# Operand addresses of four kinds of matmul products set congruent modulo 512 bytes

## The chip, the cores and the metric

The kernel runs on one core of one Trainium2 chip. The metric is device time in microseconds of one execution. The engines are TensorE (PE; its weight loads are listed apart as PEld), VectorE (DVE), ScalarE (ACT), GpSimd (POOL) and SyncE (SP, which issues DMAs). A tile lies on 128 partitions; an address here is the byte offset inside a partition of the on-chip memory (SBUF), and it is the same on all partitions.

## The reference

For tokens x (2048 x 512) the output is x + A(xn) + B(xn), where xn is the layer norm of x. A is linear attention with a learned feature map (32 heads of 16), B a gated unit whose gate mixes tokens:

```python
def _A_ref(x, wqkv, w_phi, wo):
    ...
    pq = jnp.einsum("bhsd,hdf->bhsf", q, w_phi)
    pk = jnp.einsum("bhsd,hdf->bhsf", k, w_phi)
    phi_q = jnp.concatenate([_softmax(pq, axis=-1), _softmax(-pq, axis=-1)], axis=-1)
    phi_k = jnp.concatenate([_softmax(pk, axis=-1), _softmax(-pk, axis=-1)], axis=-1)
    kv = jnp.einsum("bhsf,bhsd->bhfd", phi_k, v)
    z  = jnp.einsum("bhsf->bhf", phi_k)
    num = jnp.einsum("bhqf,bhfd->bhqd", phi_q, kv)
    den = jnp.einsum("bhqf,bhf->bhq", phi_q, z)[..., None] + 1e-6
    o = num / den
    return (...) @ wo

def _B_ref(x, w_in, w_sp, b_sp, w_out):
    z = _gelu(jnp.einsum("bsd,df->bsf", x, w_in))
    z1 = z[..., :Fh]
    z2 = _layernorm(z[..., Fh:], axis=-1)
    g = jnp.einsum("ts,bsf->btf", w_sp, z2) + b_sp[None, :, None]
    return jnp.einsum("bsf,fd->bsd", z1 * g, w_out)
```

w_in is 512 x 1376 (Fh = 688), w_sp 2048 x 2048, w_out 688 x 512.

## The kernel before

All is float32. Each product is made of three matmuls on operands split into a high and a low part: `mm3` (lines 51 to 55) issues ah·bh, ah·bl and al·bh, which are the rows of L53, L54 and L55. The first operand of a matmul is loaded as weights (128 columns), the second is streamed (344 or 512 columns). There are 16 tiles of 128 tokens.

*Phase 0* (to about 205 us). For each tile, x is centred and transposed, and split into xT (high and low); `proj` multiplies xT with wv and with wqk (q and k), 4 chunks of 128 rows each, 512 columns. A softmax pair on DVE and ACT makes e; `add_kv` adds the products of e and v into kvps (L312) after the tiles in RUNS. `z1_raw` multiplies xT with the first half of w_in (w1: two halves of 344 columns, each as h and l) into zps.

*Phase 1* (to about 284 us). The last five tiles of z1 follow; `make_zb` sums zacc over the tokens with four matmuls (pz, from zh and zl); `load_win` loads and splits the second half of w_in (w2), eight chunks of 344 columns; then z2 = xT · w2 for 16 tiles, gelu and norm, and `b_split` turns each pair of token tiles into B tiles (with sums in a tile T of the pool zw, one buffer).

*The gate's products* (to about 495 us). 32 steps of w_sp times z2 in a seven-product form (FORM: P1, P2, P6, P5, P7, P3, P4), 42 matmuls of 344 columns per step. `prep_a` prepares a step's weights: it loads wf, makes four sums in a tile S (lines 531 to 535) and splits wf and S into A tiles. After every fourth step `drain` reads the seven sums out, and the result goes through `gate` to u.

*Phase 2*. For each tile, u times w_out (wu, 512 columns, five chunks and a rest), the attention (`attend`), and its product with wo (four chunks), both into pout.

The order of instructions on each engine is set by the framework's scheduler, by its own estimate of times, among what the data, the buffers and a few explicit `issue_after` permit. So a change of buffers can move instructions that the diff does not name. SP issues its DMAs in order: one that waits for a buffer holds up those behind it.

*Addresses.* The pool xz has 16 slots of P x 2 x FH floats (5504 bytes, 10 times 512 and 384 more). xT, B, wu, u and staged tiles lie in them, so that tiles in neighbouring slots differ by 384 modulo 512, and the low half of an xT lies 2752 bytes (192 modulo 512) behind the high one. A chunk of w1 or w2 is 344 floats, 1376 bytes (352 modulo 512). The chunks of xT (128 floats) and of wv, wqk and wo (512 floats) are multiples of 512 bytes. wo's product has its two operands at the constant difference 192, the projections have one of 0, 128, 256 and 384 by tile, the wu product 128, 256 or 384 (once 0), the z and g products each of the 16 multiples of 32.

Of the kernel before, what the change touches and what calls it, by code (L numbers as in the profile page):

```python
# [10 lines left out]
F32 = mybir.dt.float32  # L11
F32R = mybir.dt.float32r
# [6 lines left out]
P = 128  # L19
# [12 lines left out]
XB = 5  # L32
NP = NT // 2
HP, QP = P // 2, P // 4


@with_exitstack
def mixer(ctx: ExitStack, tc: tile.TileContext, x, x_t, wv, wqkT, phi_bd, wo, w_in, wst, b_r, w_out, out):
# [25 lines left out]

    cst = ctx.enter_context(left("cst", 1))
    xz = ctx.enter_context(left("xz", NT))
    mid = ctx.enter_context(ExitStack())
    dram = ctx.enter_context(tc.tile_pool(name="dram", bufs=1, space=DRAM))
    e_d = dram.tile([NT, P, NF + 2 * H], F32, name="e_d")
# [96 lines left out]
    with ExitStack() as p0:  # L166
# [11 lines left out]
        wqk_h = res.tile([P, 2, ND, D], F32R, name="wqk_h")  # L178
        wqk_l = res.tile([P, 2, ND, D], F32R, name="wqk_l")
        def stage(name, dt=F32):  # L180
            return xz.tile([P, 2, FH], dt, tag="xz", name=name)

        def split_w(h, l, src, t):
            sp.dma_start(t, src)
            round_h(act, h, t)
            rest_l(l, t, h)

        bd = stage("bd")[:, 0, :D]

        def load_rows(src):  # L190
            raw = [stage("wrow") for _ in range(2)]
# [29 lines left out]
            return [[pl.tile([P, D], F32, tag=tag, name="fold").rearrange("p (c g b) -> p c g b", c=2, g=NG)  # L221
                     for _ in range(2)] for pl, tag in pools]

        w1 = [[w1_pool.tile([P, ND, FC], F32R, name=f"w1_{j}{k}") for k in "hl"] for j in range(2)]

        def load_win(dst, j, stp, tag, bufs):
            for c in range(ND):
                t = stp.tile([P, D if tag == "x" else FC], F32, tag=tag, bufs=bufs, name="wst_")
                split_w(dst[0][:, c], dst[1][:, c], w_in[c * P:(c + 1) * P, j * FC:(j + 1) * FC], t[:, :FC])

        def proj(s, wh, wl, p=None, cs_=range(ND)):
            p = ps.tile([P, D], F32, tag="mm", name="proj") if p is None else p
# [9 lines left out]
                xt[s] = load_x(s)  # L242

        def split_x(src):
            t = xz.tile([P, 2, FH], F32R, tag="xz", name="xT")
            xT.append(t)
            src = src.rearrange("p a b -> p (a b)")
            rounded.append(round_h(act, t[:, 0, :D], src))
            return rounded[-1], rest_l(t[:, 1, :D], src, t[:, 0, :D])

        def stats(s, keep=lambda **ins: None):
            st6 = wk.tile([P, 6], F32, tag="st6", name="st6")
# [35 lines left out]

        def proj_k(s):
            er = spare[s].rearrange("p a b -> p (a b)")[:, :NF + 2 * H] if s in spare else None  # L290
            return softmax_pair(wk, proj(s, wqk_h[:, 1], wqk_l[:, 1]), "k", r_x[:, s:s + 1], ebufs=3, er=er)

        def proj_q(s):
            e = softmax_pair(wk, proj(s, wqk_h[:, 0], wqk_l[:, 0]), "q", r_x[:, s:s + 1])
# [27 lines left out]
        wkT_t = load_rows.raw  # L322
        fetch(2)
        wqT = load_rows(wqkT[:D])
        fetch(3)
        w1r = [stage("w1row") for _ in range(2)]
        for c in range(ND):
# [39 lines left out]
            keep(act=i, dve=j)  # L367


        t = xz.tile([P, 2, FH], F32R, tag="xz", name="xT")  # L370
        xT.append(t)
        x0, pts = xt.pop(0), []
        for k in range(2):
# [56 lines left out]
                    keep(act=round_h(act, h, src))  # L430
                    keep(dve=rest_l(l, src, h))

        ek = [softmax_pair(wk, p, "k", r_x[:, 0:1], ebufs=3, meanwhile=split_w1)]
        proj_v(2)
        keep(pe=proj.last)
        ek.append(proj_k(1))
# [1 line left out]
        split_x(turned(3))  # L438
        z1_raw(wk, za, 0, 2)
        keep(pe=zproj.last)  # L440
        spare.update(zip((3, 4, 8, 9), wkT_t + w1r))
        n1, nq = 1, 0
        for s in range(NT):
            fetch(s + 4)
# [25 lines left out]
    ctx_zw, ctx_w2 = right("zw", 1), right("w2", 1)  # L470
    zw = ctx_zw.__enter__()
    w2_pool = ctx_w2.__enter__()
    w2 = [[w2_pool.tile([P, ND, FC], F32R, name=f"w2_{j}{k}") for k in "hl"] for j in range(2)]
    zbp_ctx = psum("zb", 1)
    zbp = zbp_ctx.__enter__()

# [40 lines left out]
    def prep_a(n, f):  # L517

        a, b = f
        pl = hl[n % 2]  # L520
        ops = {}

        def parts(names, src):
            t = pl.tile([P, 2, len(names), 2, P], F32R, tag="".join(names), name="A")
            prep_a.last = b_parts(t[:, 0], t[:, 1], src)
            for k, m in enumerate(names):
                ops[m] = t[:, 0, k], t[:, 1, k]

        sums = ws.tile([P, 4, 2, P], F32, tag="S", name="S")
        parts(("A11", "A12"), a)  # L530
        dve.tensor_tensor(sums[:, 0], b[:, 0], b[:, 1], op=ALU.add)
        dve.tensor_tensor(sums[:, 1], sums[:, 0], a[:, 0], op=ALU.subtract)  # L532
        parts(("S1", "S2"), sums[:, 0:2])
        dve.tensor_tensor(sums[:, 2], a[:, 0], b[:, 0], op=ALU.subtract)
        dve.tensor_tensor(sums[:, 3], a[:, 1], sums[:, 1], op=ALU.subtract)
        parts(("S3", "S4"), sums[:, 2:4])
        parts(("A22",), b[:, 1:2])
        return ops

    hl, raw, A = [ws, None], {}, {}  # L540
    NE = 2
    with ExitStack() as p1:
        tmp1 = p1.enter_context(left("tmp1", 1))
        kvT = tmp1.tile([P, D], F32, name="kvT")
        zb = tmp1.tile([P, NF], F32, name="zb")
        psk = p1.enter_context(psum("psk", 2))

        def make_zb():

            ones_r = tmp1.tile([P, P], F32R, name="ones_r")  # L550
            round_h(act, ones_r, ones)
            for k in range(2):
                pz = psk.tile([P, D], F32, tag="kvt", name="pz")
                cs = slice(k * D, (k + 1) * D)
                h, l = (tmp1.tile([P, D], F32R, tag="z" + n, bufs=2, name="z" + n) for n in "hl")
                round_h(act, h, zacc[:, cs])
                rest_l(l, zacc[:, cs], h)
                pe.matmul(pz, ones_r, h, start=True, stop=False)
                pe.matmul(pz, ones_r, l, start=False, stop=True)
                dve.tensor_copy(zb[:, cs], pz)  # L560

        def make_kvT():
            kvm = zw.tile([P, 4, FC], F32, tag="T", name="kvm").rearrange("p a b -> p (a b)")[:, :D]
            kvm = kvm.rearrange("p (g b) -> p g b", b=P)
            dve.tensor_tensor(kvm.rearrange("p g (k b) -> p g k b", k=2),
                              kv_acc.unsqueeze(2).to_broadcast([P, NG, 2, HP]),
                              mask.rearrange("p (k b) -> p k b", k=2).unsqueeze(1).to_broadcast([P, NG, 2, HP]),
                              op=ALU.mult)
            pt = psk.tile([P, NG, P], F32, tag="kvt", name="kvt")
            for g in range(NG):  # L570
                pe.transpose(pt[:, g], kvm[:, g], ident)
            act.activation(kvT, pt.rearrange("p g b -> p (g b)"), AF.Copy)

        with ExitStack() as p1a:
            ta = p1a.enter_context(left("tmp1a", 1))
            for j in range(2):
                load_win(w2[j], 2 + j, ta, "st", 4)
            for s in range(NT - LAG, NT):
                z1_raw(tmp1, (za, zbp)[s % 2], s, 2)
                if s == NT - LAG + 1:  # L580
                    make_zb()
            make_kvT()
            raw[0], raw[1] = load_a(0), load_a(1)
            A[0] = prep_a(0, raw.pop(0))
        sp.dma_start(kvT_d, kvT)
        sp.dma_start(zb_d, zb)
        tb = p1.enter_context(left("tmp1b", 1))
        for s in range(NE):
            et = load_q(s, tb.tile([P, QW], F32, tag="et", bufs=2, name="et"))
            tmp = zw.tile([P, 4, FC], F32, tag="z2", bufs=2, name="qtmp").rearrange("p a b -> p (a b)")[:, :NF]  # L590
            e, _ = q_fin(et, tmp, zb)
            early = sp.dma_start(e_d[s, :, :NF], e).ins
# [12 lines left out]
    def b_tile():  # L605
        nonlocal nb
        k, nb = nb, nb + 1
        shape = [P, 2, 2, FC]
        if k < 10:
            return (xz2a if k < 5 else xz2).tile(shape, F32R, tag="b", name="B")  # L610
        if k < 26:
            return xz.tile(shape, F32R, tag="xz", name="B")
        return x3[0].tile(shape, F32R, tag="b", name="B")

    B, b11 = [], None

# [60 lines left out]
    raw[2] = load_a(2)  # L677
    normed(*late.pop(), ins)
    ctx_zw.__exit__(None, None, None)
    ctx_zc.__exit__(None, None, None)  # L680
    zbp_ctx.__exit__(None, None, None)
    ctx_z.__exit__(None, None, None)
# [60 lines left out]
        return turn  # L743

    def slot(name, dt=F32):
        return xz.tile([P, 2, FH], dt, tag="xz", name=name).rearrange("p a b -> p (a b)")

    def load_w(src, parts, h, l, t):
        rows = 0
# [16 lines left out]
        return ap.rearrange("p (k b) -> p k b", b=P)  # L766

    def first_gate(i):
        a, b = slot("u_uh", F32R), slot("ul_rt", F32R)
        n = KF * P  # L770
        u = load_u(i, k_tiles(a[:, :n]).bitcast(F32), b[:2 * REM, n:n + P])
        return split_u(*u, k_tiles(a[:, n:2 * n]), k_tiles(b[:, :n]))

# [5 lines left out]
        return e  # L779

    def stage_w():
        t = [xz2.tile([P, 2, 2, FC], F32, tag="b", name="wof").rearrange("p a b c -> p (a b c)") for _ in range(3)]
        w = [slot("wu", F32R) for _ in range(KF + 1)]
        for c in range(KF + 1):
            n = P if c < KF else 2 * REM
            h, l = (w[c][:n, k * D:(k + 1) * D] for k in range(2))
            rows = [(c * P, (c + 1) * P)] if c < KF else [(KF * P, FH)] * 2
            load_w(w_out, rows, h, l, t[c // 2][:, c % 2 * D:(c % 2 + 1) * D])
            wu.append((h, l))

    g, es, ets = {}, {}, {}
    for n in range(NC):
# [26 lines left out]
            es[2], last = q_fin(ets.pop(2), slot("qtmp")[:, :NF], zb)  # L819
        if n == NC - 2:  # L820
            es[0], es[1] = first_q(0), first_q(1)
            t = slot("u1", F32R)
            us = {1: load_u(1, k_tiles(t[:, :KF * P]).bitcast(F32), t[:2 * REM, KF * P:(KF + 1) * P])}
    cb = drain(NP - 1, g, slot("c").rearrange("p (k j f) -> p k j f", k=2, j=2))
    with tc.issue_after(cb[2]):
# [109 lines left out]

    fT = attend_T(0)
    wk.tile([P, D], F32, tag="xr", bufs=3, name="xr")
    wk.tile([P, 40], F32, tag="gap", name="gap")
    wk.tile([P, NG, 2 * P], F32R, tag="oTh", name="oT")
    with tc.issue_after(lasts[5]), tc.issue_after(lasts[1]), tc.issue_after(fin[-1]):  # L940
        for c in range(ND):
# [79 lines left out]
```

## Time and profile before

| | us |
|---|---|
| median of 3 runs | 631.67 (630.98 to 631.93) |
| the profiled execution | 632.01 |
| its span | 629.9 |
| PE busy | 623.2 |
| DVE busy | 508.3 |
| ACT busy | 278.8 |
| POOL busy | 102.8 |

In a row of a group stand the line, the engine, the operation, output and inputs by the program's names without numbers, shapes and count, then busy time in us and the mean of one in ns, then idle time in front of it. In a row of the timeline stand start and duration in us. The duration of a matmul is modelled and longer than the time to the next one's start, since they overlap; times of matmuls are therefore taken from start to start. In a row of windows stand the window, its length, the busy time and number of instructions of each engine, the granted clock of TensorE (1.00 is full speed), the busy share of the DMA engines and GB/s. In a row of waits stand the instruction, what it waited for, the total in us, how often, and the longest.

### The profile page before, as it was taken

The numbers are of one execution on the slowest core, as the hardware profiler recorded it, in microseconds if no ns is written. First come the engines' busy times: TensorE is split into PE (matmuls) and PEld (weight loads), VectorE is DVE, ScalarE is ACT, GpSimd is POOL, SyncE is SP. The second block draws the span as 40 slices with busy tenths as digits, with TensorE's granted clock in tenths as the row PEclk, the third lists the DMA queues.
The fourth block names the chain that finished last, engine by engine and source line by source line (L and its number), as shares of the span: only waits on it lengthen the run. The fifth ranks groups of instructions, "written<-read, shape, count | busy, mean of one in ns | idle before, by whom it ended". The sixth has DMA issues, their size and how long they took to land.

```text
span 629.9 us, 11435 instructions
## 1 busy us (share of the span) xinstructions
PE 623.2 (99%) x4406; PEld 566.0 (90%) x4406; DVE 508.3 (81%) x893; ACT 278.8 (44%) x446; POOL 102.8 (16%) x187
## 2 busy tenths in 40 slices
PE   8999999999999999999999999999999999999997
PEld 7888888888888999999999999999999877777785
DVE  5999998988997669889989697696969899989211
ACT  5653434343332637887534344243444433334331
POOL 3142121110111005432000000000000212211110
PEclk9999999999999999999999999999999999999999
DMA  9445455345335957102463745637377799984822
GB/s 316 153 114 142 112 151 146 109 131 142 107 92 163 287 195 263 55 2 68 128 140 122 177 92 154 133 117 170 88 184 231 226 295 332 329 229 110 160 33 52
DMA packets 87590, 98.40 MB, mean 156 GB/s; under 512 B 46560, under 2 KB 59616, under 8 KB 87296
## 3 DMA queue, kind: packets, MB, share of 16 engines
q1 hardware_dynamic: 75200, 58.12, 33.0%
q0 software_dynamic: 10032, 33.92, 20.6%
q10 hardware_dynamic: 2304, 5.64, 2.4%
q8 instruction: 34, 0.56, 0.4%
q14 instruction: 20, 0.16, 0.1%
HBM read 56.37 MB, written 30.54 MB: 138 GB/s over the span
## 4 chain that ended last, share of the span: by engine, by line
PE 97%; DVE 1%; DMA 1%; issue 0%; POOL 0%; DVEq 0%; POOLq 0%
PE g L53 10%; PE g L55 10%; PE g L54 10%; PE proj L53 7%; PE proj L55 7%; PE proj L54 7%; PE zps L53 6%; PE zps L55 6%; PE zps L54 6%; PE pout L53 5%; PE pout L55 5%; PE pout L54 5%; PE ptq L879 1%; PE po L894 1%; PE kvps L312 1%; PE pout L908 1%
## 5 line engine op out<-in xcount | busy, mean ns | idle before, releaser
L54 PE MATMUL g<-B,A 128*128 128x344 f32 x448 | 143.2, 320 | 0.0
L53 PE MATMUL g<-B,A 128*128 128x344 f32 x448 | 143.1, 320 | 0.0
L55 PE MATMUL g<-B,A 128*128 128x344 f32 x448 | 142.9, 320 | 0.0
L53 PEld LDWEIGHTS g<-B,A 128*128 128x128 f32 x448 | 84.2, 188 | 0.0
L54 PEld LDWEIGHTS g<-B,A 128*128 128x128 f32 x448 | 84.2, 188 | 0.0
L55 PEld LDWEIGHTS g<-B,A 128*128 128x128 f32 x448 | 84.1, 188 | 0.0
L45 ACT ACTIVATE A<-S 128x512 fp32r<-128x512 f32 x64 | 39.3, 628 | 78.7 <-DVE S L532 60.2
L113 ACT ACTIVATE e<-e,r_x 128x1024 f32<-128x1024 f32 x28 | 32.2, 1149 | 47.1 <-DVE e L112 46.7
L53 PE MATMUL proj<-wqk_h,xT 128*128 128x512 f32 x128 | 50.9, 398 | 0.0
L55 PE MATMUL proj<-wqk_h,xT 128*128 128x512 f32 x128 | 50.6, 395 | 0.0
L54 PE MATMUL proj<-wqk_l,xT 128*128 128x512 f32 x128 | 50.3, 393 | 0.0
L49 DVE TENSOR_TENSOR A<-S,A 128x512 fp32r<-128x512 f32 x64 | 43.1, 685 | 6.5 <-ACT A L45 6.3
L45 ACT ACTIVATE A<-wf 128x512 fp32r<-128x512 f32 x64 | 33.3, 520 | 29.3 <-PE g L55 17.8
L53 PE MATMUL zps<-w_0h,xT 128*128 128x344 f32 x128 | 41.4, 323 | 0.0
L55 PE MATMUL zps<-w_0h,xT 128*128 128x344 f32 x128 | 41.1, 321 | 0.0
L53 PE MATMUL zps<-w_1h,xT 128*128 128x344 f32 x128 | 41.0, 320 | 0.0
L55 PE MATMUL zps<-w_1h,xT 128*128 128x344 f32 x128 | 40.9, 320 | 0.0
L54 PE MATMUL zps<-w_0l,xT 128*128 128x344 f32 x128 | 40.9, 319 | 0.0
L54 PE MATMUL zps<-w_1l,xT 128*128 128x344 f32 x128 | 40.9, 319 | 0.0
L116 DVE TENSOR_REDUCE sm<-e 128x64 f32<-128x1024 f32 x28 | 33.8, 1208 | 5.4 <-ACT e L113 5.4
L49 DVE TENSOR_TENSOR A<-wf,A 128x512 fp32r<-128x512 f32 x64 | 35.1, 548 | 3.1 <-ACT A L45 3.1
L696 POOL DMA_DIRECT2D z1t<-z_d x16 | 8.6, 544 | 165.1 <-DMA u_d<-z1t 127.5
(208 smaller groups left out, 1428.2 us busy)
## 6 DMA issues: line engine op xcount, KB each, us to landing
wf<-in_wst SPq DMA_DIRECT2D x64, 256.0 KB, 3.5
e_d<-e POOLq DMA_DIRECT2D x16, 544.0 KB, 5.4
et<-e_d SPq DMA_DIRECT2D x16, 544.0 KB, 6.2
zacc<-e POOLq DMA_DIRECT2D x12, 512.0 KB, 4.6
er<-et POOLq DMA_DIRECT2D x12, 512.0 KB, 5.5
z_d<-z1f ACTq DMA_DIRECT2D x16, 344.0 KB, 3.1
z1t<-z_d POOLq DMA_DIRECT2D x16, 344.0 KB, 5.1
u<-u_d SPq DMA_DIRECT2D x15, 320.0 KB, 5.2
```

Source lines behind the costliest of these rows:

```text
L45: return act.activation(h, src, AF.Copy).ins
L49: return (eng or dve).tensor_tensor(l, src, h.bitcast(F32), op=ALU.subtract).ins
L53: pe.matmul(dst, ah, bh, start=start, stop=False)
L54: pe.matmul(dst, ah, bl, start=False, stop=False)
L55: return pe.matmul(dst, al, bh, start=False, stop=stop).ins
L113: act.activation(e, e, AF.Exp, scale=scale)
L116: dve.tensor_reduce(sm, heads(e), axis=AX.X, op=ALU.add)
L312: i = pe.matmul(kv_acc[k:k + QP, m // 4], vs[:, m * QP:(m + 1) * QP], e[:, m * HP:(m + 1) * HP], start=first and m < 4 and len(ready) == n ...
L696: pool.dma_start(t[:, k, :FH], z1_d[2 * i + k])
L879: pe.transpose(pt[:, a, k].bitcast(F32R), src, ident_r)
L894: lasts[3] = pe.matmul(po[r][c * QP:(c + 1) * QP, k], kvT[rows, m // 2, cols], fs[m // 4][rows, m // 2 % 2], start=True, stop=True).ins
L908: lasts[2] = pe.matmul(p, rt, w, start=False, stop=i == NT - 1 and k == 1).ins
```

## The change

It sets the address differences of the operands of four kinds of products (projections, z, wu, wo) to multiples of 512 bytes:

- the slots of xz, and of the pools for B and for staged w_out, get 5632 bytes (11 times 512); the low half of an xT follows its high half after 2048 bytes;
- each chunk of w1 and w2 gets 384 floats of room, 1536 bytes, of which 344 are used;
- a small tile is put behind w2, and the one called gap in front of oT grows from 40 to 64 floats.

To make room for it,

- S shares the slot of T (tag "T" of zw, one buffer) for the first two steps, and gets a pool of its own behind that;
- the w2 chunks are staged in tiles of tag "z2", four to a tile;
- zh and zl become one tile zhl, which the first et later takes the place of;
- the ring of e for k has two buffers instead of three, and three more tiles use spare slots of xz.

The B operands of the g products keep their inner layout; with slots of 5632 bytes their differences to A are 448, 352, 288 and 0 for the high part, and 192 more for the low one.

```diff
+FP = 3 * P
+SL = 2 * FH + QP
...
+    def xz_tile(n, dt, name):
+        return xz.tile([P, SL], dt, tag="xz", name=name)[:, :n]
...
-        w1 = [[w1_pool.tile([P, ND, FC], F32R, name=f"w1_{j}{k}") for k in "hl"] for j in range(2)]
-
-        def load_win(dst, j, stp, tag, bufs):
+        w1 = [[w1_pool.tile([P, ND, FP], F32R, name=f"w1_{j}{k}")[:, :, :FC] for k in "hl"] for j in range(2)]
+
+        def load_win(dst, j):
+            t = zw.tile([P, 4, FC], F32, tag="z2", bufs=2, name="wst_")
             for c in range(ND):
-                t = stp.tile([P, D if tag == "x" else FC], F32, tag=tag, bufs=bufs, name="wst_")
-                split_w(dst[0][:, c], dst[1][:, c], w_in[c * P:(c + 1) * P, j * FC:(j + 1) * FC], t[:, :FC])
+                split_w(dst[0][:, c], dst[1][:, c], w_in[c * P:(c + 1) * P, j * FC:(j + 1) * FC], t[:, c])
...
-            t = xz.tile([P, 2, FH], F32R, tag="xz", name="xT")
+            t = xz_tile(2 * D, F32R, "xT").rearrange("p (a b) -> p a b", a=2)
             xT.append(t)
             src = src.rearrange("p a b -> p (a b)")
-            rounded.append(round_h(act, t[:, 0, :D], src))
-            return rounded[-1], rest_l(t[:, 1, :D], src, t[:, 0, :D])
+            rounded.append(round_h(act, t[:, 0], src))
+            return rounded[-1], rest_l(t[:, 1], src, t[:, 0])
...
-            return softmax_pair(wk, proj(s, wqk_h[:, 1], wqk_l[:, 1]), "k", r_x[:, s:s + 1], ebufs=3, er=er)
+            return softmax_pair(wk, proj(s, wqk_h[:, 1], wqk_l[:, 1]), "k", r_x[:, s:s + 1], er=er)
...
-        spare.update(zip((3, 4, 8, 9), wkT_t + w1r))
+        spare.update(zip((2, 3, 4, 5, 8, 9), [bd_t] + wkT_t + wqT_t[:1] + w1r))
...
-    w2 = [[w2_pool.tile([P, ND, FC], F32R, name=f"w2_{j}{k}") for k in "hl"] for j in range(2)]
+    w2 = [[w2_pool.tile([P, ND, FP], F32R, name=f"w2_{j}{k}")[:, :, :FC] for k in "hl"] for j in range(2)]
+    w2_pool.tile([P, QP], F32, name="gap")
...
-        sums = ws.tile([P, 4, 2, P], F32, tag="S", name="S")
+        sums = (sm[0].tile([P, 4, 2, P], F32, name="S") if sm else
+                zw.tile([P, 4, FC], F32, tag="T", name="S").rearrange("p a b -> p (a b)")[:, :8 * P].rearrange("p (a k b) -> p a k b", a=4, k=2))
...
+        zhl = tmp1.tile([P, 4, D], F32R, tag="zhl", name="zhl")
...
-                h, l = (tmp1.tile([P, D], F32R, tag="z" + n, bufs=2, name="z" + n) for n in "hl")
+                h, l = (zhl[:, 2 * k + n] for n in range(2))
...
-            et = load_q(s, tb.tile([P, QW], F32, tag="et", bufs=2, name="et"))
+            et = load_q(s, tb.tile([P, QW], F32, name="et") if s else tmp1.tile([P, 4, D], F32, tag="zhl", name="et").rearrange("p a b -> p (a b)")[:, :QW])
...
-        shape = [P, 2, 2, FC]
         if k < 10:
-            return (xz2a if k < 5 else xz2).tile(shape, F32R, tag="b", name="B")
-        if k < 26:
-            return xz.tile(shape, F32R, tag="xz", name="B")
-        return x3[0].tile(shape, F32R, tag="b", name="B")
+            t = (xz2a if k < 5 else xz2).tile([P, SL], F32R, tag="b", name="B")
+        elif k < 26:
+            t = xz_tile(SL, F32R, "B")
+        else:
+            t = x3[0].tile([P, SL], F32R, tag="b", name="B")
+        return t[:, :4 * FC].rearrange("p (a b c) -> p a b c", a=2, b=2)
...
     ctx_zw.__exit__(None, None, None)
+    sm.append(mid.enter_context(right("S", 1)))
...
-        w = [slot("wu", F32R) for _ in range(KF + 1)]
+        w = [xz_tile(2 * D, F32R, "wu") for _ in range(KF + 1)]
...
-    wk.tile([P, 40], F32, tag="gap", name="gap")
+    wk.tile([P, 2 * QP], F32, tag="gap", name="gap")
```

No engine gets more or fewer instructions. Three places move.

SP, at the end of phase 0 (wst is the staging of w2, wf the weights of a gate step, et the stored features of q). Before:

```order
L173 DMA xt<-in_x 128x512 x12
L184 DMA wst__2248<-in_w_in 128x344
L184 DMA wst__2260<-in_w_in 128x344
L513 DMA wf<-in_wst 128x512 x3
L184 DMA wst__2264<-in_w_in 128x344
L184 DMA wst__2276<-in_w_in 128x344
L513 DMA wf<-in_wst 128x512
L586 DMA zb_d<-zb 128x1024
L513 DMA wf<-in_wst 128x512 x2
L480 DMA et<-e_d 128x1088 x2
```

(between wst__2248 and wst__2260, and between wst__2264 and wst__2276, two more like them). After:

```order
L179 DMA xt<-in_x 128x512 x12
L489 DMA et<-e_d 128x1088 x2
L190 DMA wst__2245<-in_w_in 128x344 x4
L190 DMA wst__2258<-in_w_in 128x344 x4
L522 DMA wf<-in_wst 128x512 x4
L595 DMA zb_d<-zb 128x1024
```

The two loads of et stand ahead of the eight of w2 instead of behind them, and the loads of wf behind all of these.

DVE, where the sums of the second gate step, A[1], are made. Before they stand right behind the last splits of w2 (S_3262 is their tile):

```order
L49 TENSOR_TENSOR w2_1l_2233<-wst__2272,w2_1h_2232 128x344
L49 TENSOR_TENSOR w2_1l_2233<-wst__2276,w2_1h_2232 128x344
L531 TENSOR_TENSOR S_3262<-wf_2456 128x256
L534 TENSOR_TENSOR S_3262<-wf_2454,wf_2456 128x256
L532 TENSOR_TENSOR S_3262<-S_3262,wf_2454 128x256
L535 TENSOR_TENSOR S_3262<-wf_2454,S_3262 128x256
L487 TENSOR_TENSOR qtmp_2483<-et_2481,zb_2241 128x1024
```

After (S_3248 is their tile, T_3224 the one whose slot it takes, A_3254 and A_3259 what is split from it) they stand at the end of the z2 stage:

```order
L639 TENSOR_TENSOR T_3224<-z2_3080,T_3224 128x344
L51 TENSOR_TENSOR B_3234<-T_3224,B_3234 128x688
L51 TENSOR_TENSOR A_3353<-wf_3265,A_3353 128x512
L51 TENSOR_TENSOR B_3226<-z2_3173,B_3226 128x344
L51 TENSOR_TENSOR B_3237<-T_3224,B_3237 128x688
L51 TENSOR_TENSOR B_3275<-z2_3173,B_3275 128x688
L541 TENSOR_TENSOR S_3248<-wf_2443 128x256
L544 TENSOR_TENSOR S_3248<-wf_2441,wf_2443 128x256
L542 TENSOR_TENSOR S_3248<-S_3248,wf_2441 128x256
L545 TENSOR_TENSOR S_3248<-wf_2441,S_3248 128x256
L51 TENSOR_TENSOR A_3254<-S_3248,A_3254 128x512
L51 TENSOR_TENSOR A_3259<-S_3248,A_3259 128x512
```

The four sums moved behind the last reader of T_3224.

PE, at steps 1 and 2 of the gate's products; of each product (six matmuls) the first row is shown. Before, step 1 runs P1, P2, P6, P5, P7, P3, P4:

```order
L53 MATMUL g_3310<-B_2814,A_3263 128x344
L53 MATMUL g_3317<-B_2818,A_3263 128x344
L53 MATMUL g_3324<-B_2825,A_3268 128x344
L53 MATMUL g_3331<-B_2822,A_3268 128x344
L53 MATMUL g_3338<-B_2822,A_3273 128x344
L53 MATMUL g_3345<-B_2818,A_3273 128x344
L53 MATMUL g_3352<-B_2825,A_3276 128x344
```

After (g_3299, g_3306 and g_3341 are P1, P2 and P4; g_3313, g_3320, g_3327 and g_3334 are P6, P5, P7 and P3):

```order
L55 MATMUL g_3299<-B_2800,A_3249 128x344
L55 MATMUL g_3306<-B_2804,A_3249 128x344
L55 MATMUL g_3341<-B_2811,A_3262 128x344
L55 MATMUL g_3299<-B_2989,A_3353 128x344
L55 MATMUL g_3306<-B_2993,A_3353 128x344
L55 MATMUL g_3341<-B_3000,A_3366 128x344
L55 MATMUL g_3313<-B_2811,A_3254 128x344
L55 MATMUL g_3320<-B_2808,A_3254 128x344
L55 MATMUL g_3327<-B_2808,A_3259 128x344
L55 MATMUL g_3334<-B_2804,A_3259 128x344
```

P1, P2 and P4 of step 2 (A_3353, A_3366) now run ahead of P6, P5, P7 and P3 of step 1, which need the sums; from there to about step 5 products are taken in pieces, those on high parts first.

More of the change, by code (lines that the diff above doesn't have):

```diff
@@ L180, in stage @@
         def stage(name, dt=F32):
-            return xz.tile([P, 2, FH], dt, tag="xz", name=name)
+            return xz_tile(2 * FH, dt, name).rearrange("p (a b) -> p a b", a=2)
         def split_w(h, l, src, t):
@@ L186, in split_w @@
             rest_l(l, t, h)
-        bd = stage("bd")[:, 0, :D]
+        bd_t = stage("bd")
+        bd = bd_t[:, 0, :D]
         def load_rows(src):
@@ L324, in mixer @@
         wqT = load_rows(wqkT[:D])
+        wqT_t = load_rows.raw
         fetch(3)
@@ L367, in split_t @@
             keep(act=i, dve=j)
-        t = xz.tile([P, 2, FH], F32R, tag="xz", name="xT")
+        t = xz_tile(2 * D, F32R, "xT").rearrange("p (a b) -> p a b", a=2)
         xT.append(t)
@@ L431, in split_w1 @@
                     keep(dve=rest_l(l, src, h))
-        ek = [softmax_pair(wk, p, "k", r_x[:, 0:1], ebufs=3, meanwhile=split_w1)]
+        ek = [softmax_pair(wk, p, "k", r_x[:, 0:1], meanwhile=split_w1)]
         proj_v(2)
@@ L538, in prep_a @@
         return ops
-    hl, raw, A = [ws, None], {}, {}
+    hl, raw, A, sm = [ws, None], {}, {}, []
     NE = 2
@@ L572, in make_kvT @@
             act.activation(kvT, pt.rearrange("p g b -> p (g b)"), AF.Copy)
[L574 to L584, printed above, removed]
+        for j in range(2):
+            load_win(w2[j], 2 + j)
+        for s in range(NT - LAG, NT):
+            z1_raw(tmp1, (za, zbp)[s % 2], s, 2)
+            if s == NT - LAG + 1:
+                make_zb()
+        make_kvT()
+        raw[0], raw[1] = load_a(0), load_a(1)
+        A[0] = prep_a(0, raw.pop(0))
         sp.dma_start(kvT_d, kvT)
@@ L745, in slot @@
     def slot(name, dt=F32):
-        return xz.tile([P, 2, FH], dt, tag="xz", name=name).rearrange("p a b -> p (a b)")
+        return xz_tile(2 * FH, dt, name)
     def load_w(src, parts, h, l, t):
@@ L768, in first_gate @@
     def first_gate(i):
-        a, b = slot("u_uh", F32R), slot("ul_rt", F32R)
         n = KF * P
+        a, b = xz_tile(2 * n, F32R, "u_uh"), xz_tile(n + P, F32R, "ul_rt")
         u = load_u(i, k_tiles(a[:, :n]).bitcast(F32), b[:2 * REM, n:n + P])
@@ L781, in stage_w @@
     def stage_w():
-        t = [xz2.tile([P, 2, 2, FC], F32, tag="b", name="wof").rearrange("p a b c -> p (a b c)") for _ in range(3)]
-        w = [slot("wu", F32R) for _ in range(KF + 1)]
+        t = [xz2.tile([P, SL], F32, tag="b", name="wof") for _ in range(3)]
+        w = [xz_tile(2 * D, F32R, "wu") for _ in range(KF + 1)]
         for c in range(KF + 1):
@@ L821, in mixer @@
             es[0], es[1] = first_q(0), first_q(1)
-            t = slot("u1", F32R)
+            t = xz_tile((KF + 1) * P, F32R, "u1")
             us = {1: load_u(1, k_tiles(t[:, :KF * P]).bitcast(F32), t[:2 * REM, KF * P:(KF + 1) * P])}
```

## The prediction

> **What bounds the kernel now.** I read the page's busy times first, then the waits of TensorE, then the matmul groups, then start-to-start times in the timeline.
>
> ```profile
> span 629.9 us, 11435 instructions
> PE 623.2 (99%) x4406; PEld 566.0 (90%) x4406; DVE 508.3 (81%) x893; ACT 278.8 (44%) x446; POOL 102.8 (16%) x187
> PE idle L340 <- POOL ident masks.py:199: 1.8, 1, 1.8
> PE ptq L879 <- DVE c L714: 0.2, 1, 0.2
> ```
>
> PE is busy 99% of the span, and the last two rows are all that PE waited for: 2.0 us. So only two things can shorten this kernel: fewer columns (the change removes none) or a shorter time from one matmul's start to the next. And any new wait in front of PE is paid in full. Which matmuls does the change touch?
>
> ```profile
> L53 PE MATMUL proj<-wqk_h,xT 128*128 128x512 f32 x128 | 50.9, 398 | 0.0
> L53 PE MATMUL proj<-wv_h,xT 128*128 128x512 f32 x64 | 25.9, 404 | 0.0
> L53 PE MATMUL zps<-w_0h,xT 128*128 128x344 f32 x128 | 41.4, 323 | 0.0
> L53 PE MATMUL pout<-wu,uh 128*128 128x512 f32 x75 | 30.7, 410 | 0.0
> L53 PE MATMUL pout<-woh,oT 128*128 128x512 f32 x60 | 23.7, 396 | 0.0
> L53 PE MATMUL g<-B,A 128*128 128x344 f32 x448 | 143.1, 320 | 0.0
> ```
>
> Each row has two like it, for L54 and L55, and w_0h one for w_1h (buffer numbers are left out in names). So the projections are 3 x 192 = 576 matmuls, z is 3 x 2 x 128 = 768, wu 3 x 80 = 240 (with five triples of the first tile, in another group), wo 180, and g 1344. The mean of one (320 or 398 ns) is no price: its end is modelled. The price is the start-to-start time:
>
> ```profile
> 310.00:490.00 180.00, 180.00 (x1146) 1.00 0.58 145
> 225.48 0.32 PE L53 MATMUL zps<-w_1h,xT 128*128 128x344 f32 x1
> 284.04 0.32 PE L53 MATMUL g<-B,A 128*128 128x344 f32 x1
> 110.95 0.39 PE L53 MATMUL proj<-wv_h,xT 128*128 128x512 f32 x1
> 113.71 0.39 PE L53 MATMUL proj<-wqk_h,xT 128*128 128x512 f32 x1
> ```
>
> In the g stage 180 us hold 1146 matmuls, 157 ns each, at a granted clock of 1.00. From the second to the third row lie 372 z matmuls: 58.56 / 372 = 157.4 ns. A projection tile of 12 matmuls of 512 columns takes 2.76 us, 230.0 ns each.
>
> [...]
>
> **Does the start-to-start time depend on addresses?** Per triple (ah·bh, ah·bl, al·bh) I sorted the times by the residue modulo 512 bytes between the streamed operand and the loaded one, by the addresses that the pools give.
>
> ```profile
> 43.24 0.32 PE L53 MATMUL zps<-w_1h,xT 128*128 128x344 f32 x1
> 43.70 0.39 PE L53 MATMUL proj<-wqk_h,xT 128*128 128x512 f32 x1
> 280.26 0.32 PE L53 MATMUL zps<-w_1h,xT 128*128 128x344 f32 x1
> 280.72 0.32 PE L53 MATMUL zps<-w_1h,xT 128*128 128x344 f32 x1
> ```
>
> These are the first and last of the 15 undisturbed z triples at residue 0 (each row pair is one triple, 0.46 us). Their mean is 466.9 ns; residue 256 gives 468.0 (14 triples), residue 32 the worst, 475.4 (16), and all 228 together 472.2. So for 344 columns congruence is worth 5.3 ns per triple. For 512 columns it is hardly visible:
>
> ```profile
> 176.69 0.40 PE L53 MATMUL proj<-wqk_h,xT 128*128 128x512 f32 x1
> 179.46 0.40 PE L53 MATMUL proj<-wqk_h,xT 128*128 128x512 f32 x1
> 595.00 0.39 PE L53 MATMUL pout<-wu,uh 128*128 128x512 f32 x1
> 597.79 0.39 PE L908 MATMUL pout<-wu,rt 96*128 96x512 f32 x1
> 573.53 0.40 PE L55 MATMUL pout<-woh,oT 128*128 128x512 f32 x1
> 576.80 0.29 PE L879 MATMUL ptq<-zb,er 128*128 128x128 f32 x2
> ```
>
> A projection tile at residue 0 takes 2.77 us (230.8 ns each); the tile at residue 384 above took 230.0, all tiles average 231.2. Twelve wu matmuls (residues 256, 128, 256, 384) take 2.79 us (232.5 each), and 14 wo matmuls, all at the constant residue 192, 3.27 us (233.6 each). Single steps run from 0.22 to 0.24 us.
>
> **The change part by part.** *z* (w1 and w2 chunks 1536 bytes apart, h and l apart by a multiple of 512): all 16 residues become 0. 256 triples x 5.3 ns = 1.36 us; in those 15 triples the residual part was not at 0, which is at 0 now, so I take **-1.5**. Ends: -4.9 (the shortest single step, 0.15 us, for all 768: 768 x 6.4 ns) and +0.8 (the worst residue: 256 x 3.2 ns).
>
> *Projections*: from 231.2 to the residue-0 tile's 230.8, 576 x 0.4 = **-0.2**. Ends: -4.1 (0.224 each) and +1.4 (wo's 233.6).
>
> *wu*: from 232.5 towards 230.8, 240 x 1.7 = -0.4; the row at residue 0 is a projection's, so I take **-0.3** (ends -2.0 and +0.3). *wo*: from 233.6 to 230.8, 180 x 2.8 = **-0.5** (ends -1.7 and 0).
>
> *g*: the B tiles' slots grow to 5632 bytes, which leaves four residues (448, 352, 288, 0, each with its l part) instead of 16. The triples of g at those four cost 469.3, 474.8, 473.2 and 473.6, mean 472.7, against 472.2 for all 443: 448 x 0.5 = **+0.2** (ends -1.3 and +1.2, by the best and worst residue, 469.3 and 474.8).
>
> *S shares the slot of T* until step 2. Before, the sums of A[1] were made early, in a pause of VectorE, and their lows at 287.49:
>
> ```profile
> 221.73 0.42 DVE L531 TENSOR_TENSOR S<-wf 128x256 f32<-128x256 f32 x1
> 285.67 0.88 DVE L620 TENSOR_TENSOR T<-z 128x688 f32<-128x688 f32 x1
> 286.46 0.69 DVE L49 TENSOR_TENSOR A<-wf,A 128x512 fp32r<-128x512 f32 x1
> 287.06 0.51 DVE L624 TENSOR_TENSOR T<-z,T 128x344 f32<-128x344 f32 x1
> 287.49 1.28 DVE L49 TENSOR_TENSOR A<-S,A 128x512 fp32r<-128x512 f32 x2
> 288.70 0.42 DVE L49 TENSOR_TENSOR A<-wf,A 128x256 fp32r<-128x256 f32 x1
> 289.03 0.51 DVE L629 TENSOR_TENSOR T<-z,T 128x344 f32<-128x344 f32 x1
> 289.46 0.87 DVE L49 TENSOR_TENSOR B<-z,B 128x688 fp32r<-128x688 f32 x1
> 290.24 0.42 DVE L531 TENSOR_TENSOR S<-wf 128x256 f32<-128x256 f32 x1
> 290.58 0.42 DVE L534 TENSOR_TENSOR S<-wf 128x256 f32<-128x256 f32 x1
> 305.00 0.46 ACT L715 ACTIVATE c<-g 128x344 f32<-128x344 f32 x1 [0.48 <-PE g L55]
> ```
>
> VectorE runs here without a gap; from start to start a T takes 0.79 or 0.43, A<-wf 0.60 or 0.33, A<-S 0.60, a B 0.78 (0.43 for half), a sum 0.34. Now the four sums of A[1] stand behind the T readers of b_split(6). From T at 285.67 its order has three T, three A<-wf, five B, the four sums with an A<-wf, two A<-S: 1.65 + 1.53 + 3.55 + 1.70 + 1.20 = 9.6 us, so A[1]'s lows are done at 295.3. PE takes it up by running P1, P2 and P4 of steps 1 and 2 first, and asks for them 78 matmuls after 284.04, at 296.3: no wait. A[2]'s lows stand behind c, which waits for PE's own P1 and P2 of step 3 (117 matmuls after 284.04, done at 302.7) and ACT's copy (0.46): with c (0.50), a sum and A<-S they are there at 304.6. PE asks for the first of them after 124 matmuls, at 303.5. That is **+1.1**; ends 0 (c later in VectorE's order than A<-S) and 4 (the four sums, two A<-S, a T and a B all in front of PE). Queued behind that A<-S are VectorE's sums for step 3, for which PE waits next; the loads of wf on SP that wait for the S of A[1] come later too, but VectorE reaches them later still.
>
> *SP*: the two et loads come ahead of all eight w2 chunk loads, and et(0) now waits for zhl's readers.
>
> ```profile
> 198.51 0.33 SPq L184 DMA_DIRECT2D wst__2248<-in_w_in  x1
> 211.59 0.39 PE L559 MATMUL pz<-zl,ones_r 128*128 128x512 f32 x1
> 211.80:225.50 13.70, 13.70 (x90) 13.65 (x89) 10.16 (x23) 8.67 (x19) 0.00 (x0) 1.00 0.95 314
> 223.51 0.40 PE L53 MATMUL zps<-w_0h,xT 128*128 128x344 f32 x1
> ```
>
> So the w2 loads can't start before about 211.8 (211.59 is the last matmul that reads zhl), where the first started at 198.51. Two et (544 KB each), eight chunks (172 KB) and three z_d writes (344 KB) are 3.6 MB, at 314 GB/s 11.4 us: landed by 223.2, split a microsecond later. PE needs the first half at 223.5 and the second at 225.48; the second is 1.3 us early, the first some 2 us. **0**, ends 0 and 3.4 (with half of the bandwidth, SP's 2.5 MB take 16 us, and the second half is split at 228.9).
>
> *The ring of e* drops from three buffers to two: e(14) then waits for the kvps matmuls that read the buffer before it, and VectorE's softmax with it; four PSUM buffers of projections cover that for PE. **0**, up to 1 if PE ran out of those buffers. The split of w1 writes the same elements, and phase 2's order of loads changes by a place or two: **0**, PE waits for none of them now.
>
> Sum: -1.5 - 0.2 - 0.3 - 0.5 + 0.2 + 1.1 = **-1.2 us** on the profiled execution's 632.01 (span 629.9, 2.1 around it), which is 0.34 above the median; on the median 631.67 it gives **630.5**.
>
> **The rivals.** *Floors* (0.15): every congruent matmul reaches the shortest steps seen, 0.15 and 0.22 us. 4.9 + 4.1 + 2.0 + 1.7 = 12.7 saved less 1.3: 620.3; half of it, 626.6. For it: equal residues repeat their steps to a nanosecond or so, so the spread is no noise. Against: short steps of 512 columns are followed by long ones, and no tile lies under 230.0.
>
> *Addresses do nothing* (0.15): the spread is timing, and z's gain at residue 0 goes when every neighbour is alike. Then g's place and S's wait remain: 633.0. [...]
>
> *A uniform residue locks into a bad pattern* (0.15), the one that ends slower: wo is the one product with one residue throughout, and it alternates 0.236 and 0.231, the worst of the 512s. If residue 0 does so too, the projections pay 576 x 2.4 = 1.4, wu 240 x 1.1 = 0.3, z the worst residue's 0.8, wo nothing, with g and S 1.3: +3.8, 635.5. It decides once a 512-column step passes about 231.8.
>
> *A new wait in front of PE* (0.13): w2's second half behind et (up to 3.4 us at 225.5) or S at its upper end (4 at 303), with the address gains kept: 631.9 to 633.9. For it: the DMA engines are 0.95 busy in that stretch. Against: 1.3 us of slack.
>
> **How the numbers follow.** The forecast has 0.42 and lies at 629 to 632. From no change 0.2% (1.26 us, about what a measurement can tell here) is easily missed: of its 0.42 some 0.27 is faster, 0.14 the same, 0.01 slower. Floors are faster (0.15). Nothing: 0.10 same, 0.05 slower. Lock: slower but for 0.02. New wait: 0.05 same, 0.08 slower. In all 0.42 faster, 0.31 same, 0.27 slower. The range 625.0 to 634.8 leaves out the lower half of the floors and the upper half of the lock.
>
> **What would show it.** In the after profile the first and last rows of z's stage should lie 372 x 1.9 = 0.7 us closer; wo's 14 matmuls should take 3.23 us instead of 3.27; a wait of PE on A<-S near 303 of about 1 us, none at 223 to 226. Wrong if the congruent 512s leave the band of 230 to 232.5, if z's triples don't get under 468, or if the list of PE's waits has more than 2 us of new ones.

## The result and the profile after

The changed kernel takes 642.87 us (median of 6 runs, 641.82 to 643.65) against 631.56 (630.98 to 631.93): a ratio of 1.0178, 95% interval 1.0165 to 1.0192. Forecast were 630.5 us and a range up to 634.8. The profiled execution has a span of 640.2 us, 10.3 more than before. Of all executions below, one of f4_x3_kvt was disturbed (granted clock 0.85, 678.16 us) and is left out.

The page of the changed kernel: span, busy times, and of the 40 slices the rows of PE and of its granted clock.

```profile
span 640.2 us, 11431 instructions
PE 621.8 (97%) x4406; PEld 565.1 (88%) x4406; DVE 508.8 (79%) x893; ACT 280.6 (44%) x446; POOL 104.6 (16%) x187
PE   8999999999999999999999999999999399999997
PEclk9999999999999999999999999999999799999999
```

PE is busy 1.4 us less than before, in a span that is 10.3 longer. The loss lies in one slice, the 32nd (496 to 512 us), where PE is busy three tenths and its clock falls. The list of PE's waits (us in total, times, longest) names it:

```profile
PE po L905 <- ACT f L892: 9.7, 1, 9.7
PE idle L348 <- POOL ident masks.py:199: 1.8, 1, 1.8
PE g L55 <- ACT A L47: 1.1, 1, 1.1
PE pout L57 <- DVE oT L51: 0.4, 1, 0.4
PE proj L55 <- ACT wv_h L47: 0.3, 1, 0.3
PE zps L55 <- ACT z1f L149: 0.3, 1, 0.3
```

One wait of 9.7 us, of the attention product po on f, the transposed features that ScalarE copies out of PSUM. Which instruction of ScalarE was late, and for what? The timelines of PE, ScalarE and GpSimd of the changed kernel around that place:

```profile
500.51 0.64 PE L905 MATMUL po<-f,kvT 64*32 64x256 f32 x8
510.81 2.05 PE L905 MATMUL po<-f,kvT 64*32 64x256 f32 x24 [9.67 <-ACT f L892]
...
495.62 0.60 ACT L892 ACTIVATE f<-ptq 128x512 f32<-128x512 f32 x1 [3.37 <-PE ptq L890]
510.16 1.57 ACT L892 ACTIVATE f<-ptq 128x512 f32<-128x512 f32 x3 [13.95 <-DMA u_d<-z1t]
511.61 2.20 ACT L47 ACTIVATE woh<-wof 128x512 fp32r<-128x512 f32 x4
...
498.13 3.63 POOL L752 DMA_DIRECT2D u_d<-z1t  x4 [37.18 <-DVE z1t L749]
```

and of the kernel before, ScalarE and GpSimd:

```profile
496.09 2.29 ACT L881 ACTIVATE f<-ptq 128x512 f32<-128x512 f32 x4 [2.94 <-PE ptq L879]
510.80 0.60 ACT L926 ACTIVATE xr<-pout 128x512 f32<-128x512 f32 x1 [4.10 <-DMA u_d<-z1t]
...
498.89 3.63 POOL L741 DMA_DIRECT2D u_d<-z1t  x4 [36.67 <-ACT woh L45]
```

Before, ScalarE writes all four f in a row at 496.09; now it writes one, waits 13.95 us for the DMA u_d<-z1t, and writes the other three at 510.16. That DMA neither reads nor writes f: it stores the transposed gate of the last but one pair of tiles out of the tile z1t. What the two share is memory. By the addresses, z1t lies at 190944 to 196832. The five buffers of f (line 880 before) lay at 180128 to 190368, just below it; the change makes the 16 slots of xz 128 bytes longer each, all that is allocated behind them moves 16 x 128 = 2048 bytes up, and the fifth buffer of f now lies at 190368 to 192416, over z1t. The second f of the first pair of tiles uses that buffer. In the kernel before it was xr that lay over z1t and waited for the same DMA (4.10 us at 510.80), but nothing on PE waited for xr there.

PE's time from start to start, summed by group in the two traces, in us (f4 is the first experiment):

| group | before | after | f4 |
|---|---|---|---|
| projections (576 matmuls) | 136.24 | 134.46 | 134.44 |
| z with w1 (384) | 61.52 | 60.47 | 60.47 |
| z with w2 (384) | 60.53 | 61.21 | 60.67 |
| g (1344) | 211.56 | 213.52 | 214.11 |
| po (256) | 8.19 | 19.46 | 8.19 |
| wu (272, with the rest rows) | 65.17 | 65.23 | 64.58 |
| wo (180) | 42.05 | 41.85 | 41.45 |

po alone is 11.3 us longer, more than the 9.7 of the wait. Most of the rest is in the 24 po behind it: from 510.81 they take 1.98 us, where 24 of the 256 in 8.19 us are 0.77, and the granted clock is lower there. It stays at 1.00 until 503.9, is half from 504 to 514.2, and is full again behind that, as the windows of PE show (window, length, busy time and count, clock, DMA share, GB/s):

```profile
500.00:503.90 3.90, 1.14 (x11) 1.00 1.10 302
504.00:514.20 10.20, 3.39 (x27) 0.50 0.82 232
514.20:516.00 1.80, 1.80 (x9) 1.00 0.00 0
516.00:522.00 6.00, 6.00 (x28) 1.00 0.42 141
```

PE had stopped at 501.15 and resumed at 510.81, so the first 3.4 us behind the wait run at half of the clock.

### The profile page after: what moved, and what is told of

It is laid out like the page before. It is cut to its first block, busy times and chain, and to the rows that moved or that the text cites. A ratio compares the mean times of both kernels' runs of the same rounds, so it can differ in the third digit from the quotient of the medians.

```text
span 640.2 us, 11431 instructions
## 1 busy us (share of the span) xinstructions
PE 621.8 (97%) x4406; PEld 565.1 (88%) x4406; DVE 508.8 (79%) x893; ACT 280.6 (44%) x446; POOL 104.6 (16%) x187
## 4 chain that ended last, share of the span: by engine, by line
PE 88%; DMA 4%; DVE 3%; SPq 3%; issue 1%; ACT 0%; POOL 0%; DVEq 0%; ACTq 0%; POOLq 0%
PE g L55 10%; PE g L57 10%; PE g L56 10%; PE proj L57 7%; PE proj L55 7%; PE proj L56 7%; PE zps L55 5%; PE zps L56 5%; PE zps L57 5%; PE pout L55 4%; PE pout L57 4%; PE pout L56 4%; DMA et<-e_d 2%; PE ptq L890 1%; PE kvps L319 1%; PE pt L275 1%
## 5 line engine op out<-in xcount | busy, mean ns | idle before, releaser
L47 ACT ACTIVATE A<-wf 128x512 fp32r<-128x512 f32 (+1 forms) x64 | 33.2, 520 | 35.8 <-DMA wf<-in_wst 14.8
L119 ACT ACTIVATE e<-e,r_x 128x1024 f32<-128x1024 f32 x26 | 29.9, 1150 | 41.5 <-DVE e L118 41.0
L51 DVE TENSOR_TENSOR A<-wf,A 128x512 fp32r<-128x512 f32 (+1 forms) x64 | 34.9, 549 | 3.1 <-ACT A L47 2.7
L122 DVE TENSOR_REDUCE sm<-e 128x64 f32<-128x1024 f32 x26 | 31.3, 1205 | 4.4 <-ACT e L119 4.4
```

The costliest lines, as they stand in the source:

```text
L47: return act.activation(h, src, AF.Copy).ins
L51: return (eng or dve).tensor_tensor(l, src, h.bitcast(F32), op=ALU.subtract).ins
L119: act.activation(e, e, AF.Exp, scale=scale)
L122: dve.tensor_reduce(sm, heads(e), axis=AX.X, op=ALU.add)
```

## The experiments

Times are medians, each beside runs of the kernel before on the same chip (631.66 us for f4, pad, pad_f4 and s_share; 632.03 for f4_x3, f4_kvt, f4_x3_kvt and f4_r64; 631.76 for f4_x3_kvt2). pad, pad_f4, f4_kvt and f4_r64 were executed once each, so that their whole times tell only large differences; what is said of them beyond that rests on their traces.

**1. f4: the changed kernel with four buffers of f.** It takes f back below z1t, and moves all that lies behind it by another multiple of 512 bytes, so residues stay.

```diff
-            f = wk.tile([P, 2, 2 * P], F32, tag="f", bufs=NG + 1, name="f")
+            f = wk.tile([P, 2, 2 * P], F32, tag="f", bufs=NG, name="f")
```

> The changed kernel with four buffers of f instead of five; the order of all engines stays as it is. The fifth buffer lay at 190368 to 192416 and so over the tile z1t (190944 to 196832), which the last transposed gate is still read from by u_d<-z1t. Theory (the overlap makes ScalarE's second f wait for that DMA, and PE behind it): the 9.7 us wait of po on f goes, and with it the lower clock behind it, 11.3 us by the sum of PE's steps in that group: 631 to 632 us. Rival (the DMA queue or the loads of wo are late of themselves): the wait moves to another instruction near 510 and the time stays over 638 us.

630.45 us (11 runs), ratio 0.9983, interval 0.9973 to 0.9992. The 9.7 us are gone; ScalarE's timeline in f4, and PE's waits:

```profile
495.67 2.07 ACT L892 ACTIVATE f<-ptq 128x512 f32<-128x512 f32 x4 [3.17 <-PE ptq L890]
...
PE idle L348 <- POOL ident masks.py:199: 1.8, 1, 1.8
PE g L55 <- ACT A L47: 1.6, 2, 1.3
```

The four f stand in a row again. By the two ratios to the kernel before, 1.0178 and 0.9983, the overlap of f and z1t costs 0.0195 x 631.6 = 12.3 us; without it the change is some 1.1 us faster than the kernel before.

**2. pad and pad_f4: the layout alone.** The kernel before with one unused tile in front of phase 2's tiles; in pad_f4 with four buffers of f besides.

```diff
     cw = ctx.enter_context(left("cw", 1))
+    cw.tile([P, D], F32, name="pad")
```

> The kernel before with one unused tile of 2048 bytes put at the start of the pool cw, so that all tiles of phase 2 lie 2048 bytes higher, as they do in the changed kernel; orders and all operand residues stay as before. Theory (layout alone): one wait of po on f of some 9 to 10 us near 510, 641 to 643 us. Rival (the congruent addresses or the moved loads cause it): no such wait, 631.6 us.

> The kernel before with the same unused tile and four buffers of f. Theory: with f below 190944 again, no wait, 631.0 to 632.2 us. Rival (another tile of phase 2 that moved is the cause, or four buffers of f are too few): over 634 us.

pad took 644.35 us, pad_f4 631.62; the 15 executions of the kernel before lie between 631.17 and 632.95. In pad, waits of PE and ScalarE's timeline:

```profile
PE po L895 <- ACT f L882: 10.3, 1, 10.3
...
511.59 1.57 ACT L882 ACTIVATE f<-ptq 128x512 f32<-128x512 f32 x3 [14.62 <-DMA u_d<-z1t]
```

The whole loss appears in a kernel that has none of the change's edits, its residues and orders those of before, and goes when f is taken off z1t. So neither the congruent addresses nor the moved loads are its cause.

**3. s_share: S in the slot of T alone**, in the kernel before (the change's lines on sums and sm, nothing else).

> The kernel before with S in the slot of T for the first two steps and in a pool of its own after that, nothing else; PE's order stays P1, P2, P6 and so on. Theory (sums of A[1] behind T's readers cost PE a wait): PE waits 1 to 4 us between 290 and 305, 632.7 to 635.7 us. Rival (VectorE catches up in time): no wait of PE, 631.6 us.

634.65 us, ratio 1.0051 (1.0037 to 1.0065). PE's waits:

```profile
PE g L53 <- ACT A L45: 2.3, 2, 1.2
```

The g group is 3.3 us longer than before. This term of the change is real, and larger than the 1.1 us of the prediction: 2.3 us of it are the two waits, the rest slower steps around them (0.26 us at 302.69 and 302.95, where the others take 0.16).

**4. f4_x3: f4 with S of A[1] elsewhere**, in a slot of the last B tiles, which stands empty from the end of z2 to the last b_split.

```diff
         sums = (sm[0].tile([P, 4, 2, P], F32, name="S") if sm else
-                zw.tile([P, 4, FC], F32, tag="T", name="S")...
+                (x3[0].tile([P, SL], F32, tag="b", name="S") if n else
+                 zw.tile([P, 4 * FC], F32, tag="T", name="S"))[:, :8 * P]...
```

> f4 with the S of A[1] in the first slot of the last two B tiles (free from the end of the z2 stage to the last b_split) instead of in the slot of T. In f4 two waits of PE on A<-S near 303 to 307, with the slow first steps behind them, cost 2.4 us of the g group. Theory (T's slot holds the sums up): no wait of PE in the g stage, 627.8 to 628.6 us. Rival (VectorE has too much to do in that stretch wherever S lies): the waits stay, 630.4 us.

628.85 us (4 runs), ratio 0.9942 (0.9922 to 0.9962): slower than expected by up to 1 us. The waits in g are gone and its sum is 211.81 us, 2.30 less than in f4. That is 0.25 more than in the kernel before, which is what the new residues of B and the new order of the products cost together. But the runs spread from 627.4 to 630.93, and the profiled one, the slowest, has a wait that f4 had not; PE's first wait and VectorE's timeline:

```profile
PE pout L57 <- DVE oT L51: 2.7, 1, 2.7
...
521.78 1.23 DVE L496 TENSOR_TENSOR qtmp<-et,zb 128x1024 f32<-128x1024 f32 x1 [2.89 <-DMA et<-e_d]
```

Phase 2 starts earlier than in f4, and in this execution VectorE waited there for a load of et. That this explains the spread of the other three runs was not shown, since they have no trace.

**5. f4_kvt: what stands ahead of z2.** Transposes of kvT before the four 512-column matmuls of make_zb, into a PSUM tile of the pool za, and no w2 matmul ahead of the last one of w1.

```diff
-            pt = psk.tile([P, NG, P], F32, tag="kvt", name="kvt")
+            pt = za.tile([P, D], F32, tag="z", name="kvt").rearrange("p (g b) -> p g b", b=P)
...
+                with tc.issue_after(kvt_last[0]):
+                    pe.matmul(pz, ones_r, h, start=True, stop=False)
...
+                make_kvT()
                 make_zb()
-        make_kvT()
...
+        with tc.issue_after(zproj.last):
+            p = zproj((kv_ps_p, zc, zbp, za)[s % 4], s, w2, (0, 1) if s % 2 == 0 else (1, 0))
```

> f4 with the transposes of kvT ahead of the four matmuls of make_zb (512 columns, streamed operand at a constant residue), so that from these to the end of z2 only matmuls of 344 columns at residue 0 follow one another; before, two transposes stood right ahead of z2. In f4 z runs at 153.3 ns each behind projections and at 157.8 behind transposes and kvps, and stays at one of the two until something else runs. Theory (two steady patterns, the matmuls ahead choose): z2 runs at 153.3, 384 x 4.5 = 1.7 us less, 628.8 us. Rival (w2's own addresses or the load of that stage set it): z2 stays at 157.8, 630.5 us.

The mechanism holds, the time does not follow: 631.64 us. The first row of each pair is the first matmul of z2's second tile, the second row the first of the g products, in f4 and then in f4_kvt:

```profile
224.27 0.32 PE L55 MATMUL zps<-w_1h,xT 128*128 128x344 f32 x1
281.07 0.32 PE L55 MATMUL g<-B,A 128*128 128x344 f32 x1
```

```profile
224.77 0.32 PE L55 MATMUL zps<-w_1h,xT 128*128 128x344 f32 x1
279.97 0.32 PE L55 MATMUL g<-B,A 128*128 128x344 f32 x1
```

360 matmuls take 56.80 us in f4, 157.8 ns each, and 55.20 in f4_kvt, 153.3 each, with the same operands at the same residues. z2 is 1.79 us shorter in all; z1 is 0.62 longer, 0.5 of it a wait for z1f (list of waits in f4_kvt). PE reaches the g products 1.1 us earlier, but VectorE begins the sums of S for the third step at 300.72 instead of 299.72, and PE waits more often:

```profile
PE g L55 <- ACT A L47: 1.3, 1, 1.3
PE g L55 <- ACT B L47: 0.6, 1, 0.6
PE g L56 <- DVE B L51: 0.5, 1, 0.5
```

At the last of these waits the granted clock fell to half, and g's steps became 287 ns long. First two windows of PE, then two of the steps:

```profile
284.00:302.30 18.30, 16.04 (x96) 1.00 0.18 55
302.40:305.70 3.30, 3.17 (x11) 0.50 0.66 226
303.27 0.49 PE L55 MATMUL g<-B,A 128*128 128x344 f32 x1
303.56 0.49 PE L56 MATMUL g<-B,A 128*128 128x344 f32 x1
```

g is 2.86 us longer than in f4. The waits make 0.8 of that (2.4 us against 1.6); some ten steps at half of the clock make about 1.3 (estimated from 287 against 158 ns). Only the first of the three waits is for a split of S, which held PE up in f4 too; the two for B are new. One execution doesn't show whether the clock falls each time.

**6. f4_x3_kvt: both**, run twice, the second time as f4_x3_kvt2, whose trace is the one used.

> Both edits, of f4_x3 and f4_kvt. If both theories hold, 626.2 to 627.0 us; if one of them, 628 to 629; if none, 630.5.

> The same kernel as f4_x3_kvt once more, to see its traces undisturbed. By the groups of f4_x3 and f4_kvt: g at its sum of before (211.6 to 212.0 us) with no wait on A<-S, z2 at 153.3 ns each; a wait of one of wo's products on oT of up to 2.7 us near 520, for a DMA of et that lands late, in some executions. 626.5 to 628.7 us. Rival (the gains of f4_x3 and f4_kvt don't add): 629 us or more.

628.02 us, ratio 0.9936 (0.9922 to 0.9950), and 628.57, ratio 0.9937 (0.9923 to 0.9951). It is the fastest here, with f4_x3 (0.9942) inside its interval: the two gains don't add to the 626.2 to 627.0 us of the first expectation. The second trace is of the slowest of its six executions (630.25 us). z2 runs at 153.3 ns there (58.88 us, 1.79 less than in f4), but z1 takes 0.62 us more, as in f4_kvt, and PE waits for oT and for A:

```profile
PE pout L57 <- DVE oT L51: 1.9, 1, 1.9
PE idle L348 <- POOL ident masks.py:199: 1.8, 1, 1.8
PE g L55 <- ACT A L47: 1.1, 1, 1.1
```

The wait on A<-S, which f4_x3 had lost, is there again, and g takes 213.51 us, not the 211.6 to 212.0 of the second expectation. VectorE begins these sums at 298.34, later than in f4_x3 (296.92), while PE comes earlier.

**7. f4_r64: another constant residue.** 64 bytes in front of w1 and 64 more behind w2, so that projections and z1 lie at 64 and z2 at 448.

```diff
+    w1_pool.tile([P, 16], F32, name="shift")
...
-    w2_pool.tile([P, QP], F32, name="gap")
+    w2_pool.tile([P, QP + 16], F32, name="gap")
```

> f4 with the operands of projections and z1 at the constant residue 64 and those of z2 at 448, by 64 bytes put in front; wu and wo stay at 0. Theory (residue 0 is what makes the short pattern): projections at 230 ns or more instead of 226.7, z1 at 156 or more instead of 153.3 to 157.8, together 2.5 to 4 us more, 633 to 634.5 us. Rival (any constant residue does): projections at 226.7 as in f4, 630.5 us.

631.53 us, between the two expectations; the steps tell more. A projection tile of 12 matmuls, the last of tile 15, first and next row, in f4 and then in f4_r64:

```profile
192.81 0.39 PE L55 MATMUL proj<-wqk_h,xT 128*128 128x512 f32 x1
195.53 0.32 PE L55 MATMUL zps<-w_0h,xT 128*128 128x344 f32 x1
```

```profile
194.40 0.40 PE L55 MATMUL proj<-wqk_h,xT 128*128 128x512 f32 x1
197.20 0.32 PE L55 MATMUL zps<-w_0h,xT 128*128 128x344 f32 x1
```

2.72 us, 226.7 ns each, at residue 0; 2.80 us, 233.3 each, at 64. This tile is one of the slower ones: at 64 the projections settle at either of two paces, 229 ns (about two thirds of them) or 233.3. Over all, projections take 1.33 us more than in f4 and z1, at 156.0 ns, 0.52 more, while z2 at 448 stays at its 60.67. So being constant isn't enough for the products of 512 columns: of the constant residues that they were run at (0, 64, and 192 in wo before, 233.6 ns), 0 alone has the 226.7 ns. For z2, residue 448 does no worse than 0, and what stands ahead of it counts for more (1.79 us in experiment 5). The expectation of 2.5 to 4 us was too high, since it put all projections at 230 ns or more.

## Why the prediction was wrong, point by point

*The step that failed* is the one that read "phase 2's order of loads changes by a place or two: 0, PE waits for none of them now". It looked at the order of phase 2 and not at its addresses. The slots of xz grow by 2048 bytes in all, the prediction used that growth for residues, and didn't follow it to what lies behind them. The row that could have raised the question stood in the trace of before: xr's wait of 4.10 us for u_d<-z1t, a DMA that has nothing to do with xr's data and so tells of a shared place in memory. Experiments 1 and 2 show this step to be worth 12.3 us; without it the forecast of 630.5 meets f4's 630.45.

*That this agrees so well* is partly luck, as the terms (f4's group against before) show:

| term | forecast | measured |
|---|---|---|
| z (w1 and w2) | -1.5 | -0.9 |
| projections | -0.2 | -1.8 |
| wu | -0.3 | -0.6 |
| wo | -0.5 | -0.6 |
| g: S in T's slot (measured: f4 against f4_x3) | +1.1 | +2.3 |
| g: B's residues (measured: f4_x3 against before) | +0.2 | +0.25 |

*Projections* were under-sized: the row taken (the tile at residue 0, 230.8 ns) had its low part at 192; with both parts at 0 the step came to 226.7 in f4. *z* was under-sized for w1 (-1.05) and had the wrong sign for w2 (+0.14): it was forecast from 15 single triples, as if a residue gave one time, but at residue 0 f4 has two, 153.3 and 157.8 ns. *S* had the right mechanism and half of its size: the wait in g came to 1.6 us (list of waits in f4), the rest is slower steps right around the waits (0.26 to 0.27 us at 301.78 and 302.54 in the changed kernel). *B's residues*, *wo* and *wu* were close; B's figure has the new order of the products in it.

*The loads of et ahead of w2* cost nothing, as forecast: in the list of waits of the changed kernel stands no z product that waits for w2. *The ring of e* shows no wait of PE either.

*The rivals*: "floors" came true in part only: z1 came to 153.3 ns and the projections to 226.7 where nothing interrupts them, against floors of 0.15 and 0.22 us, z2, wu and wo not throughout, and the whole is far from 12.7 us. "Addresses do nothing" fell, by f4 against f4_r64: with an offset of 64 bytes the projections settle at 229 or 233.3 ns instead of 226.7. "A uniform residue locks into a bad pattern" was right for z2 (157.8 ns), wrong for all else. "A new wait in front of PE" is the one that came true in kind, by a mechanism that it didn't name.

*The signs*: the wait on A<-S of about 1 us near 303 came (1.1 us in the changed kernel). z's rows didn't move closer, since z2 didn't gain. Two of the signs of being wrong came as well: the products of 512 columns left the band of 230 to 232.5 ns, on its good side (226.7), and the list of PE's waits has more than 2 us of new ones.

## What to carry to other kernels

A change of a buffer's size is a change of every address behind it: list which tiles share memory with tiles that a DMA still reads, before and after, not only what the change means to move. Here u_d<-z1t took 6.0 to 9.1 us from issue to landing in the changed kernel. A wait for a DMA that has nothing to do with the waiting instruction's data was the mark of such a place: 13.95 us of f after, and 4.10 us of xr before, where it cost PE nothing yet. And when PE is the bound, a shorter stage brings its end earlier for all others: here z2 gained 1.79 us, against which there stood, in f4_kvt, waits for the splits of A and B (2.4 us in all) and 3.3 us at half of the clock behind them, and in f4_x3_kvt2 a wait of 1.1 us for the split of A and one of 1.9 us of one of wo's products for oT.

## What the runs showed of the hardware

A chain of matmuls with 128 x 128 weight loads and both operands at the same residue modulo 512 bytes settled, in f4, into steady steps: 226.7 ns for 512 columns (227, 227, 226 in turn), after up to eleven uneven ones behind transposes, kvps or slow z products. With 344 columns it had two steady states, 153.3 ns (153, 153, 154) and 157.8 (155 to 160 in turn), and stayed in the one in which it started: behind projections in f4 it was the first, behind transposes and kvps the second, and with four matmuls of 512 columns ahead of it (experiment 5) all of z2 ran in the first. At a difference of 64 bytes (f4_r64) it was the 512 columns that had two (229 and 233.3), and the 344 one (156.0). What makes the states was not shown. In the changed kernel the granted clock fell to 0.50 at 504.0, during 9.7 us without matmuls (501.15 to 510.81), and came back at 514.2, 3.4 us after they went on; in f4_kvt waits of 2.4 us in all were followed by 0.50 for 3.3 us (302.40 to 305.70).
